# Building a kernel's rotation tables early, in bf16, and starting the first slab before the tables are complete

## The chip, the cores and the metric

The kernel runs on one core of one Trainium2 chip. The metric is the time of one execution on the device, in microseconds (us). The record marks each run as fast or slow; a run is slow when it is over 1.5% above the fastest of the same kernel.

The engines are called by the profile's short names: PE (TensorE, matrix multiplication), DVE (VectorE, elementwise work), ACT (ScalarE, activations), POOL (GpSimd) and SP (SyncE, used here for issuing DMA). The *span* is the time from the first to the last instruction of the profiled execution.

## The reference, cut to what matters

```python
def _A_ref(x, Lambda_re, Lambda_im, B_re, B_im, C_re, C_im, log_dt, Dskip):
    Lam = Lambda_re + 1j * Lambda_im
    dt = jnp.exp(log_dt)
    Lam_bar = jnp.exp(dt * Lam)                            # 512 complex factors
    B_bar = ((Lam_bar - 1.0) / Lam)[:, None] * (B_re + 1j * B_im)
    Bu = jnp.einsum("bld,pd->blp", x + 0j, B_bar)
    for t in range(L):                                     # L = 2048 steps
        h = Lam_bar[None, :] * h + Bu[:, t, :]
        ...
    return 2.0 * jnp.einsum("blp,dp->bld", hseq, Cmat).real + x * Dskip
def _B_ref(x, w_gate, w_up, w_down):                       # 512 -> 1376 -> 512
    return (_gelu(x @ w_gate) * (x @ w_up)) @ w_down

xn = _layernorm(x)                                         # x: 1 x 2048 x 512, bf16
return x + _A_ref(xn, ...) * _silu(_B_ref(xn, ...))
```

The complex recurrence is the sequential part. The kernel writes `Lam_bar` as a radius `rho` times a rotation. It rotates the inputs of each step backwards by the angle that has gathered, so that the scan itself is real with the factor `rho`, and rotates the results forwards again. For this it needs tables over the 512 positions of a slab: cosine and sine, and the same rotation multiplied by `2 (Lam_bar - 1) / Lam`, which is called `W`.

## The kernel before

The sequence is cut into four slabs of 512 positions. A prologue loads everything, computes the layernorm and builds the tables. Then, for each slab, eleven blocks of the feed-forward network (FFN) are interleaved with four scan groups, one for each 128 states. The cuts are marked with `# ...`.

```python
prolo_cm = tc.tile_pool(name="prolo", bufs=1)
prolo = prolo_cm.__enter__()                 # memory that is given back after the prologue
xT = prolo.tile([P, KT, S], BF16, name="xT")
# ... parameters, x (transposed while it is loaded) and the weights are fetched by DMA
for c in range(NSLAB):                       # layernorm statistics
    # ... mean_ps: matmuls of xT with ones
    x2 = prolo.tile([P, KT, TS], BF16, name="x2", tag="x2", bufs=2)
    nc.vector.tensor_tensor(out=x2[:], in0=xT[:, :, cols], in1=xT[:, :, cols], op=ALU.mult)
    # ... msq_ps: matmuls of x2 with ones; m2 = mean^2; var = msq - m2; mean_b; lnv; rstd_b
emit_xn(0)                                   # xnT = (xT - mean_b) * rstd_b, two DVE ops per 128x512
# ... dt_, th, a1, rho, c0, s0; then the 4-wide arithmetic that gives cr2, ci2
ang  = prolo.tile([P, NPT, TB], FP32, name="ang")        # TB = 64
ctab = prolo.tile([P, NPT, TS], FP32, name="ctab")
stab = prolo.tile([P, NPT, TS], FP32, name="stab")
# ... ctab, stab = sin/cos of ang for the first 64 columns, by ACT
while width < TS:                            # 64 -> 128 -> 256 -> 512 columns
    for pt in range(NPT):
        nc.vector.tensor_scalar(out=tmp_tab[:, 0:width], in0=stab[:, pt, 0:width], ...)
        nc.vector.scalar_tensor_tensor(out=ctab[:, pt, width : 2 * width], ...)
        nc.vector.tensor_scalar(out=tmp_tab[:, 0:width], in0=ctab[:, pt, 0:width], ...)
        nc.vector.scalar_tensor_tensor(out=stab[:, pt, width : 2 * width], ...)
    # ... the angle is doubled, width *= 2
nc.vector.tensor_copy(out=cos_b[:], in_=ctab[:])         # fp32 -> bf16, 128 x 2048
nc.vector.tensor_copy(out=sin_b[:], in_=stab[:])
for pt in range(NPT):                        # Wre_b and Wim_b, 512 columns each, from fp32
    # ... two tensor_scalar and two scalar_tensor_tensor
nc.vector.tensor_scalar(out=nWre_b[:], in0=Wre_b[:], scalar1=-1.0, ...)
nc.vector.tensor_scalar(out=nWim_b[:], in0=Wim_b[:], scalar1=-1.0, ...)
# ... diagI
for c in range(1, NSLAB):
    emit_xn(c)
prolo_cm.__exit__(None, None, None)          # the working pools below reuse prolo's memory
up  = ctx.enter_context(tc.tile_pool(name="up", bufs=4))
gel = ctx.enter_context(tc.tile_pool(name="gel", bufs=2))    # zb, sq, arg, sg, ub, zu
gp  = ctx.enter_context(tc.tile_pool(name="gp", bufs=2))     # fb, sf, g
# ... further working pools

def ffn_j(s, j, at):
    # ... g_ps: 4 matmuls
    nc.scalar.activation(out=zb[:fs], in_=g_ps[:fs, :], func=AF.Copy)
    nc.scalar.activation(out=sq[:fs], in_=g_ps[:fs, :], func=AF.Square, scale=math.sqrt(A_GELU))
    nc.vector.scalar_tensor_tensor(out=arg[:fs], in0=sq[:fs], scalar=1.0, in1=zb[:fs], ...)
    nc.scalar.activation(out=sg[:fs], in_=arg[:fs], func=AF.Sigmoid, scale=2.0 * C_GELU)
    # ... u_ps: 4 matmuls, ub = copy of it by ACT
    nc.vector.tensor_tensor(out=zu[:fs], in0=zb[:fs], in1=ub[:fs], op=ALU.mult)
    nc.vector.tensor_tensor(out=at[:fs, j, :], in0=sg[:fs], in1=zu[:fs], op=ALU.mult)

def down_m(s, m, at, gs, xs):
    # ... f_ps (2 buffers): 11 matmuls; xres is loaded
    nc.scalar.activation(out=fb[:], in_=f_ps[:, :], func=AF.Copy)
    nc.scalar.activation(out=sf[:], in_=f_ps[:, :], func=AF.Sigmoid)
    nc.vector.tensor_tensor(out=g[:], in0=fb[:], in1=sf[:], op=ALU.mult)
    gs.append(g)                             # y_epi reads g, after the y_ps matmuls

for s in range(NSLAB):
    for kind, idx in inter:                  # 3 FFN, scan, 3 FFN, scan, 3 FFN, scan, 2 FFN, scan
        if kind == "ssm":
            ssm_pt(s, idx, hst)              # p, wre, wim, fre, fim (scans), q, hst
        else:
            ffn_j(s, idx, at)
    # ... down_m and y_epi of the slab before
# ... down_m and y_epi of the last slab
```

## Time and profile before

| | kernel before |
|---|---|
| time, median of 5 runs | 286.31 us (285.25 to 286.47) |
| span of the profiled run | 283.0 us |
| DVE busy / idle in the span | 242.5 us / 40.5 us |
| first xnT written by DVE | 35.92 us |
| first FFN result zb on ACT | 72.64 us |
| last slab's scans done, g of the tail | 253.68 us |

The first view is the page's summary of the kernel before. Its first line gives busy microseconds, share of the span and instruction count for each engine. The rows of digits below it are the busy share in tenths, in 40 equal slices of 7.1 us.

```profile
PE 193.6 (68%) x880; PEld 85.4 (30%) x880; DVE 242.5 (86%) x610; ACT 145.7 (51%) x272; POOL 1.0 (0%) x8
...
PE   0058070000598898898898799789969988908993
...
DVE  0136499999699999999999999999999999999444
ACT  0218960000787585678576458757636697412420
```

DVE is full from the sixth slice to near the end, with a dip at 71 to 78 us (slice 11). It starts nearly empty, and PE and ACT stand still from about 42 to 73 us.

The second view, of the same kernel, is busy time by stage. The columns are the stretch in us, its length, then busy us and instruction count for PE, PEld, DVE, ACT and POOL, the granted PE clock, the DMA share and GB/s. The stages are: until the first xnT; the rest of the prologue; the body; the tail.

```profile
0.00:35.92 35.92, 9.98 (x32) 3.81 (x33) 11.37 (x36) 15.85 (x23) 0.98 (x8) 0.91 0.88 181
35.92:73.75 37.83, 5.35 (x16) 1.93 (x16) 36.78 (x123) 5.12 (x12) 0.00 (x0) 0.59 0.23 65
73.75:253.68 179.93, 155.47 (x716) 69.10 (x716) 177.29 (x423) 118.27 (x227) 0.00 (x0) 0.98 0.04 13
253.68:283.00 29.32, 22.78 (x116) 10.59 (x115) 17.09 (x30) 6.51 (x12) 0.00 (x0) 0.91 0.17 55
```

In the start DVE works for 11.4 of 35.9 us. In the second stage it is busy for 36.8 of 37.8 us, while PE and ACT do little. The body is DVE time, 177.3 of 179.9 us.

The third view is the timeline of DVE before, cut to the waits that matter: start, duration, engine and line, operation, result and sources, shapes, count, and in brackets the idle time just before it and what ended that.

```profile
18.90 2.36 DVE L125 TENSOR_TENSOR x<-xT 128x2048 bf16<-128x2048 bf16 x2 [10.20 <-DMA xT<-in_A_x_dram]
...
29.27 0.69 DVE L134 TENSOR_TENSOR var<-msq_ps,m 128x512 f32<-128x512 f32 x1 [2.88 <-ACT m L132]
...
35.92 0.76 DVE L150 TENSOR_TENSOR xnT<-xc,rstd_b 128x512 bf16<-128x512 bf16 x2 [3.76 <-ACT rstd_b L143]
...
71.66 0.74 DVE L290 SCALAR_TENSOR_TENSOR Wim_b<-stab,cr,wtmp 128x512 bf16<-128x512 f32 x1
...
73.75 0.69 DVE L410 SCALAR_TENSOR_TENSOR arg<-sq,zb 128x512 bf16<-128x512 bf16 x1 [0.63 <-ACT sq L408]
...
76.67 0.42 DVE L424 TENSOR_TENSOR at<-sg,zu 128x512 bf16<-128x512 bf16 x1 [1.89 <-ACT sg L414]
```

DVE stands idle for 10.2 us because x has not landed, while the table work that does not need x lies behind it in the program. At 71.66 us the last prologue operation runs that reads a tile of the prologue's pool; it ends at 72.40.

The fourth view is the first FFN activation on ACT, from the timeline of ACT before.

```profile
72.64 0.60 ACT L406 ACTIVATE zb<-g_ps 128x512 bf16<-128x512 f32 x1 [32.70 <-issue]
```

Its matmuls were done at about 41.7 us, yet zb came at 72.64, 0.24 us after the last read of the prologue's pool. The profile names no engine for the 32.7 us ("issue"). The reading is that the instruction waited for memory to come free; E2 below tests it.

### The profile page before, as it was taken

How to read it: one execution, taken by the hardware profiler on the slowest of the kernel's cores; microseconds unless marked ns; L12 is line 12 of the kernel's file. 1: busy time of each engine (PE TensorE's matmuls, PEld its weight loads, DVE VectorE, ACT ScalarE, POOL GpSimd, SP SyncE). 2: the span in 40 equal slices, each digit the busy share in tenths (PEclk: the TensorE clock that was granted, in tenths of full speed). 3: DMA queues.
4: the chain of work that ended last, by engine and by line, in shares of the span. 5: the costliest groups of instructions: out<-in, count | busy, mean ns of one | idle time of the engine just before them, and what ended most of it. 6: DMA issues, size and time to landing. Idle time of an engine off the chain costs nothing.

```text
span 283.0 us, 2919 instructions
## 1 busy us (share of the span) xinstructions
PE 193.6 (68%) x880; PEld 85.4 (30%) x880; DVE 242.5 (86%) x610; ACT 145.7 (51%) x272; POOL 1.0 (0%) x8
## 2 busy tenths in 40 slices
PE   0058070000598898898898799789969988908993
PEld 0013020000243343343353344334424433403441
DVE  0136499999699999999999999999999999999444
ACT  0218960000787585678576458757636697412420
POOL 1000000000000000000000000000000000000000
PEclk9999568555599999999999999999999999977999
DMA  7999448000000000000000040000004000001301
GB/s 81 283 234 208 95 108 257 0 0 0 0 5 0 0 0 0 2 0 1 0 2 1 0 127 22 2 0 0 0 2 140 9 0 0 3 0 37 111 21 57
DMA packets 26224, 12.81 MB, mean 45 GB/s; under 512 B 19712, under 2 KB 25184, under 8 KB 26208
## 3 DMA queue, kind: packets, MB, share of 16 engines
q1 hardware_dynamic: 21520, 10.17, 14.6%
q10 hardware_dynamic: 4688, 2.46, 3.9%
q8 instruction: 7, 0.11, 0.2%
q14 instruction: 9, 0.07, 0.1%
HBM read 6.33 MB, written 2.10 MB: 30 GB/s over the span
## 4 chain that ended last, share of the span: by engine, by line
DVE 53%; issue 16%; ACT 13%; PE 9%; DMA 6%; SPq 2%; ACTq 1%; DVEq 0%
DVE fre L360 7%; DVE fim L363 7%; DVE at L424 4%; DMA xT<-in_A_x_dram 4%; DVE arg L410 4%; PE y_ps L451 4%; DVE zu L423 4%; PE f_ps L435 4%; DVE p L344 2%; ACT zb L406 2%; ACT sg L414 2%; ACT ub L421 2%; DVE p L349 2%; DVE wre L345 2%; ACT sq L408 2%
## 5 line engine op out<-in xcount | busy, mean ns | idle before, releaser
L402 PE MATMUL g_ps<-xnT,wg 128*128 128x512 bf16 (+1 forms) x176 | 47.0, 389 | 49.7 <-ACT sq L408 39.3
L435 PE MATMUL f_ps<-wd,at 128*128 128x512 bf16 (+1 forms) x176 | 44.0, 385 | 13.0 <-ACT sf L441 11.7
L406 ACT ACTIVATE zb<-g_ps 128x512 bf16<-128x512 f32 (+1 forms) x44 | 26.7, 606 | 46.7 <-issue 32.7
L417 PE MATMUL u_ps<-xnT,wu 128*128 128x512 bf16 (+1 forms) x176 | 47.1, 390 | 4.2 <-ACT uim L339 3.7
L414 ACT ACTIVATE sg<-arg 128x512 bf16<-128x512 bf16 (+1 forms) x44 | 28.0, 636 | 28.6 <-DVE arg L410 28.4
L402 PEld LDWEIGHTS <-wg 128*128 128x128 bf16 (+1 forms) x176 | 17.7, 101 | 73.9 <-issue 57.1
L451 PE MATMUL y_ps<-C,hst 128*128 128x512 bf16 x128 | 31.7, 384 | 0.6 <-DVE hst L389 0.6
L410 DVE SCALAR_TENSOR_TENSOR arg<-sq,zb 128x512 bf16<-128x512 bf16 (+1 forms) x44 | 30.1, 684 | 0.8 <-ACT sq L408 0.6
L435 PEld LDWEIGHTS <-at 128*128 128x128 bf16 (+1 forms) x176 | 17.0, 98 | 34.0 <-DVE q L388 12.4
L421 ACT ACTIVATE ub<-u_ps 128x512 bf16<-128x512 f32 (+1 forms) x44 | 27.3, 620 | 0.0
L408 ACT ACTIVATE sq<-g_ps 128x512 bf16<-128x512 f32 (+1 forms) x44 | 26.8, 610 | 0.0
L417 PEld LDWEIGHTS <-wu 128*128 128x128 bf16 (+1 forms) x176 | 18.0, 102 | 26.7 <-issue 7.9
L439 ACT ACTIVATE fb<-f_ps 128x512 f32<-128x512 f32 x16 | 9.7, 604 | 23.1 <-DVE g L443 13.3
L424 DVE TENSOR_TENSOR at<-sg,zu 128x512 bf16<-128x512 bf16 (+1 forms) x44 | 18.6, 424 | 2.4 <-ACT sg L414 2.4
L423 DVE TENSOR_TENSOR zu<-zb,ub 128x512 bf16<-128x512 bf16 (+1 forms) x44 | 18.6, 422 | 0.0
L121 PE MATMUL mean_ps<-xT,onesK 128*128 128x512 bf16 x16 | 6.0, 499 | 17.0 <-DMA xT<-in_A_x_dram 17.0
L451 PEld LDWEIGHTS <-hst 128*128 128x128 bf16 x128 | 12.3, 99 | 14.9 <-issue 1.6
L326 PE MATMUL u_re_ps<-xnT,BreT 128*128 128x512 bf16 x64 | 16.5, 380 | 0.1
L332 PE MATMUL u_im_ps<-xnT,BimT 128*128 128x512 bf16 x64 | 16.4, 379 | 0.0
L363 DVE TENSOR_TENSOR_SCAN fim<-rho,init_im,wim 128x512 bf16<-128x512 f32 x12 | 15.4, 1282 | 0.0
L360 DVE TENSOR_TENSOR_SCAN fre<-rho,init_re,wre 128x512 bf16<-128x512 f32 x12 | 15.4, 1281 | 0.0
L463 DVE TENSOR_TENSOR yg<-y_ps,g 128x512 f32<-128x512 f32 x16 | 10.8, 688 | 5.3 <-PE y_ps L455 5.3
(111 smaller groups left out, 266.7 us busy)
## 6 DMA issues: line engine op xcount, KB each, us to landing
xres<-in_A_x_dram SPq DMA_DIRECT2D x16, 128.0 KB, 2.5
out_dram<-ot SPq DMA_DIRECT2D x16, 128.0 KB, 1.7
wu<-in_B_w_up_dram ACTq DMA_DIRECT2D x1, 1376.0 KB, 6.9
wg<-in_B_w_gate_dram SPq DMA_DIRECT2D x1, 1376.0 KB, 8.1
wd<-in_B_w_down_dram SPq DMA_DIRECT2D x1, 1280.0 KB, 7.0
wd<-in_B_w_down_dram SPq DMA_DIRECT2D x1, 96.0 KB, 6.7
BreT<-in_A_B_re_dram SPq DMA_TRANSPOSE x4, 6.2
BimT<-in_A_B_im_dram SPq DMA_TRANSPOSE x4, 2.7
```

The costliest lines, as they stand in the source:

```text
L360: nc.vector.tensor_tensor_scan(out=fre[:], data0=rho_b_ap, data1=wre[:], initial=ire, op0=ALU.mult, op1=ALU.add)
L363: nc.vector.tensor_tensor_scan(out=fim[:], data0=rho_b_ap, data1=wim[:], initial=iim, op0=ALU.mult, op1=ALU.add)
L402: nc.tensor.matmul(g_ps[:fs, :], lhsT=wg[:, kt, fsl], rhs=xnT[:, kt, cols], start=(kt == 0), stop=(kt == KT - 1))
L406: nc.scalar.activation(out=zb[:fs], in_=g_ps[:fs, :], func=AF.Copy)
L408: nc.scalar.activation(out=sq[:fs], in_=g_ps[:fs, :], func=AF.Square, scale=math.sqrt(A_GELU))
L410: nc.vector.scalar_tensor_tensor(out=arg[:fs], in0=sq[:fs], scalar=1.0, in1=zb[:fs], op0=ALU.add, op1=ALU.mult)
L414: nc.scalar.activation(out=sg[:fs], in_=arg[:fs], func=AF.Sigmoid, scale=2.0 * C_GELU)
L417: nc.tensor.matmul(u_ps[:fs, :], lhsT=wu[:, kt, fsl], rhs=xnT[:, kt, cols], start=(kt == 0), stop=(kt == KT - 1))
L421: nc.scalar.activation(out=ub[:fs], in_=u_ps[:fs, :], func=AF.Copy)
L423: nc.vector.tensor_tensor(out=zu[:fs], in0=zb[:fs], in1=ub[:fs], op=ALU.mult)
L435: nc.tensor.matmul(f_ps[:, :], lhsT=at[:fs, k, m0 : m0 + P], rhs=wd[:fs, k, :], start=(k == 0), stop=(k == NFT - 1))
L451: nc.tensor.matmul(y_ps[:, :], lhsT=hst[:, j, m0 : m0 + P], rhs=C2[:, j, :], start=(j == 0), stop=False)
```

## The change

The intent is to use the time in which DVE waits for x, and not to let the first slab wait for the tables. The change has five parts.

1. The parameters come first and the table work is written ahead of the statistics. Fences (`issue_after`) keep the scheduler to this order on ACT and DVE.
2. The tables are bf16 from the start. `cos`, `sin`, `-Wre` and `-Wim` are all doubled from 64 to 512 columns, instead of building `W` at 512 columns from fp32 `cos` and `sin`, casting, and negating. `Wre` itself is no longer needed: `q1` gets the other sign, and an addition becomes a subtraction.
3. The table tiles no longer lie in the prologue's pool, so they don't hold its memory.
4. The remaining doublings are written after slab 0's eleven FFN blocks, and slab 0's four scan groups follow.
5. The activations are grouped by function (Exp, Sin, Ln, Exp), which cuts ACT's table loads from 8 to 5.

```diff
+        nc.sync.dma_start(out=pb[:, 2 * NPT : 3 * NPT], in_=A_log_dt.rearrange(...))
         nc.sync.dma_start(out=pb[:, NPT : 2 * NPT], in_=A_Lambda_im.rearrange(...))
         ...
+    def emit_tables_early():
+        # dt_, th, a1, rho, c0, s0, then m2cr, m2ci (= -2 times what cr2, ci2 held), ang: as before, but in consts
+        nc.scalar.activation(out=cos_b[:, :, 0:TB], in_=ang[:], func=AF.Sin, bias=halfpi[:], scale=1.0)
+        nc.scalar.activation(out=sin_b[:, :, 0:TB], in_=ang[:], func=AF.Sin)
+        # nWre_b, nWim_b at 64 columns: 16 small operations
+        tmpA = consts.tile([P, TS // 2], BF16, name="tmpA")
+        tmpB = consts.tile([P, TS // 2], BF16, name="tmpB")
+        pairs = [(cos_b, sin_b, tmpA), (nWre_b, nWim_b, tmpB)]
+        def double_to(limit):
+            ...                      # the loop of before, for both pairs, in bf16
+        double_to(2 * TB)
+        last_dve = nc.cur_bb.bb.instructions[-1]
+        return double_to, last_act, last_dve
+    double_to, last_act, last_dve = emit_tables_early()
+    def emit_tables_late():
+        double_to(TS)
+        ...                          # diagI
     for c in range(NSLAB):
         ...
-        nc.vector.tensor_tensor(out=x2[:], in0=xT[:, :, cols], in1=xT[:, :, cols], op=ALU.mult)
+        with tc.issue_after(last_dve):
+            nc.vector.tensor_tensor(out=x2[:], in0=xT[:, :, cols], in1=xT[:, :, cols], op=ALU.mult)
         ...                          # Ln, Exp and Copy regrouped with issue_after
     emit_xn(0)
-    ...                              # the old table code in prolo, cast, W builds, negations, diagI
     for c in range(1, NSLAB):
         emit_xn(c)
     prolo_cm.__exit__(None, None, None)
     ...
-        nc.vector.tensor_tensor(out=q1[:], in0=Wre_b[:, pt, :], in1=fre[:], op=ALU.mult)
+        nc.vector.tensor_tensor(out=q1[:], in0=nWre_b[:, pt, :], in1=fre[:], op=ALU.mult)
         nc.vector.tensor_tensor(out=q2[:], in0=nWim_b[:, pt, :], in1=fim[:], op=ALU.mult)
-        nc.vector.tensor_tensor(out=hst[:, pt, :], in0=q1[:], in1=q2[:], op=ALU.add)
+        nc.vector.tensor_tensor(out=hst[:, pt, :], in0=q2[:], in1=q1[:], op=ALU.subtract)
     ...
+        if s == 0:
+            for j in range(NFT):
+                ffn_j(0, j, at)
+            emit_tables_late()
+            for pt in range(NPT):
+                ssm_pt(0, pt, hst)
+        else:
             for kind, idx in inter:
                 ...
```

## The prediction

> **What bounds it now.** The stretch table (busy time by window) shows VectorE busy for 10.0, 9.7 and 9.9 us of the three 10 us windows from 40 to 70, 19.85 of 20 from 80 to 100, and 50.00 of 50 in each window from 100 to 250. So: a start (first xnT write at 35.9 us), a VectorE-bound body to 253.8, a TensorE tail of 29 us. From 35.9 to 73.75 the body is prologue. The wait view has one 32.7 us wait of ScalarE before the first zb, labelled "issue", and one 32 us wait of TensorE for sq. I read it as the prologue pool's memory: the working tiles reuse it, so the first zb must wait until the last prologue tile (tables, xT) has been read.
>
> **What changes, on VectorE.**
> Start-to-start costs read from the timeline: 512-wide bf16 tensor_tensor 0.335 us, scalar_tensor_tensor 0.20/0.26/0.39/0.66 at 64/128/256/512, fp32 tensor_scalar 0.16/0.19/0.26/0.40.
> - The 37.8 us from 35.9 to 73.75 holds 30 layernorm operations (10.1 us, kept) and 27.7 us of table work, small operations and a 0.6 us wait.
> - After: the tables at 64 and 128 columns are made while VectorE waited for x and statistics. What must be done late is 19 of 32 operations at 128 columns (3.9 us), 32 at 256 (8.8) and small ones (1.3): 14 us. This uses about 0.17 us for a 256-wide bf16 tensor_scalar, an estimate from the Trainium skill, "VectorE: DVE Perf Modes", side-by-side table (four elements per cycle; the trace's 2048-wide bf16 negation, 0.69 us, agrees).
> - The late tables no longer sit in the prologue pool, so its memory comes free at the last xnT, about 46 us, and slab 0's FFN (11 x 1.28 = 14.1 us of VectorE) runs among the table work.
>
> **The start.** ScalarE's table loads fall from 8 to 5 at 1.28 us each (Trainium skill, "ScalarE: Activation LUTs", what a load costs: 1283 ns; trace agrees). But early tables occupy VectorE until about 23.4 us, so the squares of x start there, not at 18.9. I expect this to cancel: first rstd near 35.5, first xnT after the statistics near 36 (35.9 before).
>
> **Sum.** 36.2 + 10.1 (layernorm) + 14.0 (tables) + 14.1 (FFN 0) + 1.5 bubbles (cold TensorE clock, sigmoid load) = 75.9 us, when slab 0's scans begin. Before, the body after 73.75 lasted 180.0 us, with 2.5 of start bubbles and 14.1 of slab 0's FFN: 163.4 remain, so the body ends at 239.3; plus the unchanged 29.2 tail gives a span of 268.5, some 14.5 us less. Nearly all is on the critical path: VectorE is saturated. Predicted time 271.8 us, range 267 to 276.5. Chances: faster by over 2% 0.95, within 2% 0.04, slower 0.01.
>
> **What would show it.** First zb near 46 us instead of 72.6; the 32 us waits gone; TensorE busy from 46 on; VectorE busy total lower by 8 to 14 us; first xnT near 36; VectorE saturated from about 36 to 239; tail 29 us.
>
> **What would make it wrong.** (a) Early tables delay the statistics more than the saved table loads help: first xnT at 38 to 40 costs that much one for one. (b) Slab 0's FFN alone, with two buffers and in-order table work between arg, zu and at, or a cold TensorE, leaves VectorE idle for more than 1.5 us. (c) The four scan groups in a row starve on f_ps or on ure/uim. (d) bf16 tensor_scalar with a per-partition scalar runs slower than assumed (up to 2 us). (e) The tail grows through a lower clock.

## The result, and the profile after

| | before | after |
|---|---|---|
| time, median (range, runs) | 286.29 us (285.25 to 287.17, 16) | 267.51 us (266.08 to 268.59, 9) |
| span of the profiled run | 283.0 us | 265.5 us |
| DVE busy / idle in the span | 242.5 / 40.5 us | 242.4 / 23.1 us |
| first xnT / first zb | 35.92 / 72.64 us | 33.64 / 43.95 us |
| g of the tail, and from there to the end | 253.68 / 29.3 us | 234.78 / 30.7 us |

The ratio of the times is 0.9351, with a 95% interval from 0.9331 to 0.9370. A ratio in this document is the record's ratio of one kernel's fast runs to those of the kernel before in the same rounds. It differs from the ratio of the medians quoted by up to 0.0007.

The summary of the page after, with the same rows as before:

```profile
PE 198.1 (75%) x880; PEld 86.8 (33%) x880; DVE 242.4 (91%) x654; ACT 142.1 (53%) x269; POOL 1.0 (0%) x8
...
PE   0037372999988658996987998797799789239992
...
DVE  0699999999999999999999999999999999997254
ACT  0605823999474406577474748666458758130410
```

Read the two DVE entries side by side. The busy time is the same to 0.1 us, 242.5 against 242.4; the row of digits is full from the third slice (6.6 us each) instead of the sixth. So the 17.5 us of span are idle time of DVE that is gone (40.5 - 23.1 = 17.4), not work that is gone.

Busy time by stage after. The stages are: until the first xnT; the layernorm; late tables with slab 0's FFN; the body from the first scan operation of slab 0; the tail.

```profile
0.00:33.64 33.64, 8.84 (x32) 3.48 (x33) 24.01 (x112) 14.34 (x26) 0.98 (x8) 1.00 0.85 187
33.64:43.70 10.06, 5.27 (x16) 1.96 (x16) 10.06 (x31) 1.52 (x3) 0.00 (x0) 0.83 0.56 135
43.70:71.75 28.05, 26.04 (x111) 11.30 (x111) 28.05 (x95) 25.41 (x49) 0.00 (x0) 0.94 0.15 49
71.75:234.78 163.03, 133.77 (x607) 59.03 (x606) 163.03 (x394) 94.27 (x180) 0.00 (x0) 0.96 0.05 14
234.78:265.50 30.72, 24.18 (x116) 11.08 (x115) 17.26 (x30) 6.51 (x12) 0.00 (x0) 0.88 0.17 52
```

The start is 2.3 us shorter and holds 24.0 us of DVE work instead of 11.4: the 12.6 us more, nearly all table work, were fitted in where DVE had waited. The idle time of DVE in the start falls from 24.55 to 9.63 us, so 14.9 of the 17.4 us are here: 12.6 filled with work and 2.3 from the shorter start. From 33.64 to 234.78 DVE has no idle time at all. Until the end of the tables, without the 14.1 us of slab 0's FFN, DVE does 24.01 + 10.06 + 28.05 - 14.1 = 48.0 us of work after, and 11.37 + 36.78 = 48.2 us before.

The timeline of DVE after, at the places shown of before:

```profile
21.59 1.23 DVE L274 TENSOR_TENSOR x<-xT 128x2048 bf16<-128x2048 bf16 x1
...
25.23 0.70 DVE L284 TENSOR_TENSOR var<-msq_ps,m 128x512 f32<-128x512 f32 x1
...
33.64 0.76 DVE L302 TENSOR_TENSOR xnT<-xc,rstd_b 128x512 bf16<-128x512 bf16 x2 [1.01 <-ACT rstd_b L292]
...
43.03 0.76 DVE L302 TENSOR_TENSOR xnT<-xc,rstd_b 128x512 bf16<-128x512 bf16 x2
...
45.07 0.69 DVE L409 SCALAR_TENSOR_TENSOR arg<-sq,zb 128x512 bf16<-128x512 bf16 x1
...
47.99 0.42 DVE L423 TENSOR_TENSOR at<-sg,zu 128x512 bf16<-128x512 bf16 x1
```

The waits of 10.20, 2.88, 0.63 and 1.89 us are gone, and that for rstd fell from 3.76 to 1.01. The pool's last reader is now the last xnT, which ends at 43.79, and the timeline of ACT shows the first zb 0.16 us after it:

```profile
43.95 0.60 ACT L405 ACTIVATE zb<-g_ps 128x512 bf16<-128x512 f32 x1 [8.79 <-issue]
```

Why is the busy time the same, although the large fp32 operations are gone? The groups of DVE instructions by line answer it. The columns are line, operation, names, shapes, count, busy us, mean ns and idle time before. These are three of the table groups before:

```profile
L232 DVE SCALAR_TENSOR_TENSOR ctab<-ctab,cw,tmp_tab 128x64 f32<-128x64 f32 (+2 forms) x12 | 4.6, 380 | 0.1
L225 DVE TENSOR_SCALAR tmp_tab<-stab,sw 128x64 f32<-128x64 f32 (+2 forms) x12 | 3.7, 306 | 0.1
...
L283 DVE SCALAR_TENSOR_TENSOR Wre_b<-ctab,cr,wtmp 128x512 bf16<-128x512 f32 x4 | 3.0, 748 | 0.0
```

And these are two of the groups after, the same step of a doubling:

```profile
L223 DVE SCALAR_TENSOR_TENSOR cos_b<-cos_b,cw,tmpA 128x64 bf16<-128x64 bf16 (+2 forms) x12 | 4.5, 374 | 0.0
...
L219 DVE TENSOR_SCALAR tmpA<-sin_b,sw 128x64 bf16<-128x64 bf16 (+2 forms) x12 | 3.1, 261 | 0.0
```

In bf16 the scalar_tensor_tensor of a doubling costs what it cost in fp32 (374 against 380 ns on average); only the tensor_scalar got cheaper (261 against 306). But twice as many tables are doubled, 96 operations instead of 48. The sum of the table groups' durations was 16.6 (doublings) + 9.8 (W) + 2.4 (casts) + 1.4 (negations) = 30.2 us before, and is 30.4 (doublings) + 4.2 (W at 64 columns) = 34.6 us after. Neighbouring instructions overlap in these sums, by about 0.09 us whatever their width: at 64 columns a tensor_scalar lasts 0.24 us and the next one starts after 0.15, at 512 columns a build of `W` lasts 0.75 and the next starts after 0.67. There are 112 table operations after and 68 before, so overlap takes back about 4 us of the 4.4 us that the sums differ by (44 x 0.09, an estimate), and DVE's time comes out nearly even.

Finally the gap of PE at the head of the tail, in the timeline of PE before:

```profile
255.53 1.87 PE L435 MATMUL f_ps<-wd,at 128*128 128x512 bf16 x4 [7.89 <-ACT sf L441]
257.29 2.39 PE L451 MATMUL y_ps<-C,hst 128*128 128x512 bf16 x8
```

and in the timeline of PE after:

```profile
236.62 1.86 PE L434 MATMUL f_ps<-wd,at 128*128 128x512 bf16 x4 [8.97 <-ACT sf L440]
238.38 3.57 PE L450 MATMUL y_ps<-C,hst 128*128 128x512 bf16 x8
```

After a longer gap the same eight matmuls take 3.57 instead of 2.39 us. From 5 to 10 us after the tail's g the granted clock is 0.75 after and 1.00 before. The tail's 116 matmuls keep PE busy for 24.18 instead of 22.78 us, which is the tail's extra 1.4 us.

### The profile page after: what moved, and what is told of

Read it like the earlier page. It is cut to its first block, busy times and chain, and to the rows that moved or that the text cites. A ratio compares the mean times of both kernels' runs of the same rounds, so it can differ in the third digit from the quotient of the medians.

```text
span 265.5 us, 2957 instructions
## 1 busy us (share of the span) xinstructions
PE 198.1 (75%) x880; PEld 86.8 (33%) x880; DVE 242.4 (91%) x654; ACT 142.1 (53%) x269; POOL 1.0 (0%) x8
## 4 chain that ended last, share of the span: by engine, by line
DVE 73%; PE 9%; ACT 8%; issue 4%; ACTq 3%; DMA 1%; DVEq 0%
DVE fim L362 7%; DVE fre L359 7%; DVE arg L409 6%; DVE at L423 5%; DVE zu L422 5%; PE y_ps L450 5%; PE f_ps L434 4%; ACTq L82 3%; DVE p L343 2%; DVE xnT L302 2%; DVE p L349 2%; DVE p L348 2%; DVE wre L344 2%; DVE q L386 2%; DVE g L442 2%
## 5 line engine op out<-in xcount | busy, mean ns | idle before, releaser
L401 PE MATMUL g_ps<-xnT,wg 128*128 128x512 bf16 (+1 forms) x176 | 48.6, 397 | 20.0 <-ACT sq L407 13.2
L434 PE MATMUL f_ps<-wd,at 128*128 128x512 bf16 (+1 forms) x176 | 45.4, 387 | 18.8 <-ACT sf L440 12.2
L450 PE MATMUL y_ps<-C,hst 128*128 128x512 bf16 x128 | 34.8, 414 | 0.9 <-DVE hst L388 0.9
L407 ACT ACTIVATE sq<-g_ps 128x512 bf16<-128x512 f32 (+1 forms) x44 | 26.7, 607 | 0.0
L438 ACT ACTIVATE fb<-f_ps 128x512 f32<-128x512 f32 x16 | 9.6, 598 | 27.1 <-DVE g L442 14.1
L269 PE MATMUL mean_ps<-xT,onesK 128*128 128x512 bf16 x16 | 5.1, 472 | 19.0 <-DMA xT<-in_A_x_dram 17.8
L450 PEld LDWEIGHTS <-hst 128*128 128x128 bf16 x128 | 13.0, 105 | 16.5 <-issue 4.0
L337 ACT ACTIVATE ure<-u_re_ps 128x512 bf16<-128x512 f32 x16 | 9.7, 604 | 15.1 <-PE u_re_ps L325 7.9
L462 DVE TENSOR_TENSOR yg<-y_ps,g 128x512 f32<-128x512 f32 x16 | 10.7, 687 | 7.0 <-PE y_ps L454 7.0
```

What stands on the lines that cost most here:

```text
L401: nc.tensor.matmul(g_ps[:fs, :], lhsT=wg[:, kt, fsl], rhs=xnT[:, kt, cols], start=(kt == 0), stop=(kt == KT - 1))
L434: nc.tensor.matmul(f_ps[:, :], lhsT=at[:fs, k, m0 : m0 + P], rhs=wd[:fs, k, :], start=(k == 0), stop=(k == NFT - 1))
L450: nc.tensor.matmul(y_ps[:, :], lhsT=hst[:, j, m0 : m0 + P], rhs=C2[:, j, :], start=(j == 0), stop=False)
```

## The experiments

Two theories fit the profile after, and the prediction had made a third:

- IDLE: DVE paces the kernel, and the gain is the idle time at its start that is now filled with table work.
- OVERLAP: the gain is that ACT and PE start slab 0 about 28 us earlier, because the pool's memory comes free at 43.8 instead of 72.4 us.
- LESS WORK: the gain is that the new tables cost DVE fewer microseconds. The prediction's expected fall of DVE's busy total says this, though its sum does not rest on it.

All eight kernels gave correct results. Each was timed in three rounds (four runs each, with the profiled one) beside the kernel before, which had medians of 285.71 us (E1 to E4) and 286.41 us (E4b to E7).

### E1: the early tables without the early start of slab 0

In the changed kernel the late doublings are written before the prologue's pool is closed, two of their tiles are put back into that pool, and slab 0 gets the mixed order of the other slabs.

```diff
-        tmpA = consts.tile([P, TS // 2], BF16, name="tmpA")
-        tmpB = consts.tile([P, TS // 2], BF16, name="tmpB")
+        tmpA = prolo.tile([P, TS // 2], BF16, name="tmpA")
+        tmpB = prolo.tile([P, TS // 2], BF16, name="tmpB")
     ...
+    emit_tables_late()
     prolo_cm.__exit__(None, None, None)
     ...
-        if s == 0: ... else: ...
+        for kind, idx in inter: ...      # slab 0 like the others
```

> The changed kernel with all of its table work before the prologue pool closes (the two doubling temporaries lie in that pool, the late tables are emitted before it is released, slab 0 uses the old mixed order), so ScalarE and TensorE wait for the tables again, as they did in the kernel before; VectorE's work is the same. Theory IDLE (VectorE paces the body; what the change won is VectorE idle time in the start, filled with table work): only the start-up bubbles of about 3 us come back, 269.5 to 272 us, ratio to before about 0.945, VectorE busy 242. Theory OVERLAP (what the change won is that ScalarE and TensorE start slab 0 some 28 us earlier): most of the 18.8 us is lost, 280 us or more.

Measured: 272.35 us (271.52 to 273.46), ratio 0.9539 (0.9496 to 0.9581), span 269.9 us. The start is the same as in the changed kernel (squares at 21.57, first xnT at 33.61). The timelines of ACT and DVE of this kernel show that the wait for the pool is back, and so are the bubbles (short waits of DVE) at the start of slab 0, while PE runs at 0.50 of its clock (57.5 to 62.5 us) and ACT loads the sigmoid's table (59.92 us):

```profile
57.84 0.60 ACT L406 ACTIVATE zb<-g_ps 128x512 bf16<-128x512 f32 x1 [22.70 <-issue]
```

```profile
58.95 0.69 DVE L410 SCALAR_TENSOR_TENSOR arg<-sq,zb 128x512 bf16<-128x512 bf16 x1 [0.86 <-ACT sq L408]
...
61.87 0.43 DVE L424 TENSOR_TENSOR at<-sg,zu 128x512 bf16<-128x512 bf16 x1 [1.89 <-ACT sg L414]
```

What follows: 13.1 of the 17.5 us of span come without any early start of slab 0. ACT waits 22.7 us for the pool, and the span is only 4.4 us longer than that of the changed kernel, 3.5 of them such bubbles on DVE (some smaller ones beside the two shown). The time is 0.35 us over the upper end of what IDLE expected and 7.6 us under what OVERLAP expected.

### E2: the early start of slab 0 without the early tables

In the kernel before, all tiles of the table work are moved out of the prologue's pool; nothing else is changed.

```diff
-    ctab = prolo.tile([P, NPT, TS], FP32, name="ctab")
-    stab = prolo.tile([P, NPT, TS], FP32, name="stab")
+    ctab = consts.tile([P, NPT, TS], FP32, name="ctab")
+    stab = consts.tile([P, NPT, TS], FP32, name="stab")
     # ... likewise iota_i, iota_f, ang, thT, cw, sw, tmp_tab, sq_tmp, wtmp
```

> The kernel before with every table tile moved out of the prologue pool, nothing else: the first zb no longer waits for the tables, only for the last read of xT. VectorE's work and its start are unchanged. IDLE: only the 3 us of start-up bubbles in VectorE's stream go, 282.5 to 285 us. OVERLAP: most of the gain appears here, 275 us or less.

Measured: 280.21 us (279.65 to 280.59), ratio 0.9802 (0.9774 to 0.9830), span 278.8 us. The first zb is at 53.47 us, 0.16 us after the pool's last reader (an xnT that ends at 53.31), in the timeline of ACT:

```profile
53.47 0.60 ACT L406 ACTIVATE zb<-g_ps 128x512 bf16<-128x512 f32 x1 [13.70 <-issue]
```

The stretch from 54 to 80 us in the table of busy time by stage, first for the kernel before and then for this one (DVE is the third of the busy columns):

```profile
54.00:80.00 26.00, 6.23 (x20) 2.35 (x20) 22.50 (x47) 7.33 (x14) 0.00 (x0) 0.55 0.00 0
```

```profile
54.00:80.00 26.00, 16.88 (x55) 6.48 (x57) 25.86 (x56) 12.37 (x23) 0.00 (x0) 0.69 0.00 1
```

What follows: PE does 10.7 us more in this stretch and ACT 5.0 us more, and the span gains 4.2 us, of which 3.4 are the idle time of DVE that goes away in this very stretch. Both theories missed the time: IDLE expected 282.5 us or more, so it is off by over 2 us, OVERLAP by over 5. The early start is worth about 2% (1.7 to 2.3% by the interval).

E1 and E2 are the two halves of the change, and their ratios multiply to 0.9539 x 0.9802 = 0.935, which is the ratio of the whole change, 0.9351. In spans, 13.1 + 4.2 = 17.3 of 17.5 us. E1's half still holds several parts together: the early tables, their bf16 arithmetic and the grouped activations.

### E3: the new tables, but little of them early

In the changed kernel, `W` at 64 columns and the first doubling are moved to the late part; the squares of x no longer wait for them.

```diff
+        last_dve = nc.cur_bb.bb.instructions[-1]     # now right after thT
-        double_to(2 * TB)
-        last_dve = nc.cur_bb.bb.instructions[-1]
     def emit_tables_late():
+        build_w()                                    # nWre_b, nWim_b at 64 columns
         double_to(TS)
```

> The changed kernel with the W tables at 64 columns and the doublings to 128 taken out of the start and made late; the grouped Exp, Sin, Ln, Exp order of ScalarE stays. About 8.5 us of VectorE work (14.2 to 21.5 and a little more) leave the time in which it would wait for x. IDLE: squares of x start near 18 instead of 21.6, first xnT 2.5 to 3.5 us earlier (near 30.5), body 8 us longer: 271 to 274 us. Theory LESS WORK (as the prediction had it: fewer VectorE microseconds in the tables is the gain, their place is not): within 1 us of the changed kernel or faster, 264 to 268.5 us.

Measured: 273.22 us (272.38 to 273.97), ratio 0.9558 (0.9523 to 0.9593), span 270.5 us. DVE is busy for 241.6 us, 0.8 less than in the changed kernel, and the kernel is still 5.0 us of span longer. The squares of x and the first xnT come earlier (18.41 and 31.16 us), and the wait for x is back in the timeline of DVE:

```profile
18.41 2.36 DVE L276 TENSOR_TENSOR x<-xT 128x2048 bf16<-128x2048 bf16 x2 [7.60 <-DMA xT<-in_A_x_dram]
```

What follows: the same arithmetic in the same precision loses 5 us when it isn't in the window where DVE waits for x. LESS WORK expected at most 268.5 us and falls; IDLE expected 271 to 274 and holds. But E3 also keeps 12.5 of the 17.5 us of span, and not all of that is the pool of E2. Its squares start only 0.5 us before those of the kernel before (18.41 and 18.90 us), yet its first xnT comes 4.8 us earlier (31.16 and 35.92 us). Between the two, ACT loads tables twice in E3, and five times at 1.28 us in the kernel before. So writing the parameters' activations first and grouping them (parts 1 and 5) is a likely source of some 4 us, and would also explain why the early tables did not delay the first xnT. No run tests it alone.

### E4 and E4b: the old arithmetic in the new places

E4 takes the changed kernel and puts the old fp32 arithmetic into it. `ctab` and `stab` are doubled to 256 columns early; the last doubling, the casts, the four `W` builds and the two negations come late, and all their tiles lie outside the prologue's pool.

```diff
-        pairs = [(cos_b, sin_b, tmpA), (nWre_b, nWim_b, tmpB)]
+        pairs = [(ctab, stab, tmpA)]                 # fp32
-        double_to(2 * TB)
+        double_to(4 * TB)
     def emit_tables_late():
         double_to(TS)
+        build_w()                                    # casts, W at 512 columns, negations
```

> The changed kernel's placement with the old table algorithm: fp32 cosine and sine doubled to 256 columns early, the last doubling, two casts, four W builds and two negations late. VectorE's table work in the two traces has about the same sum. IDLE: VectorE busy 242 to 245 us, 266 to 270 us. LESS WORK: the fp32 tables cost 10 us or more, 277 us or more, with VectorE busy 10 us higher than in the changed kernel.

Measured: 275.74 us (275.51 to 276.04), ratio 0.9648 (0.9622 to 0.9673), span 273.4 us: between the two expectations. The experiment was spoiled. The scheduler put the first subtraction of the layernorm ahead of early doublings, and DVE stood idle for 6.7 us until its mean was there:

```profile
21.55 0.43 DVE L310 TENSOR_TENSOR xc<-xT,mean_b 128x512 bf16<-128x512 bf16 x1 [6.69 <-ACT mean_b L304]
```

E4b repairs this with one more fence.

```diff
-            nc.vector.tensor_tensor(out=xc[:], in0=xT[:, kt, cols], in1=mean_b[:, c, :], op=ALU.subtract)
+            with tc.issue_after(last_dve):
+                nc.vector.tensor_tensor(out=xc[:], in0=xT[:, kt, cols], in1=mean_b[:, c, :], op=ALU.subtract)
```

> The run with the old fp32 table algorithm in the new placement, with the mean subtractions held behind the early doublings, so that VectorE no longer sits idle for 6.7 us in the start. IDLE: VectorE busy again 242 to 243.5, span shorter by 5 to 6.7 us than without the fence, so 269 to 271 us. LESS WORK: the earlier 275.7 was the price of the fp32 tables, so 274.5 us or more.

Measured: 272.37 us (271.68 to 273.78), ratio 0.9517 (0.9475 to 0.9558), span 270.6 us: again between the two, 1.4 us above what IDLE expected and 2.1 below what LESS WORK expected. DVE is busy for 243.0 us, only 0.6 more than with the new arithmetic. The other 4.5 of the 5.1 us of span are idle time, and the largest new piece of it is in the start, in the timeline of DVE:

```profile
19.40 1.23 DVE L283 TENSOR_TENSOR x<-xT 128x2048 bf16<-128x2048 bf16 x1 [0.36 <-DMA xT<-in_A_x_dram]
...
25.28 0.69 DVE L293 TENSOR_TENSOR var<-msq_ps,m 128x512 f32<-128x512 f32 x1 [3.06 <-PE msq_ps L286]
```

What follows: the old arithmetic itself is hardly dearer for DVE. The 3.06 us are not a lack of early table work either: right after the wait, at 25.89 us, DVE goes on with doublings at 128 columns whose inputs had been ready before it. They stand behind `var` in DVE's order, as the scheduler left it. So E4b, too, carries a wait that is not the arithmetic's. The old arithmetic does leave its casts and `W` builds for late, since they need the finished tables, while the new one can start on `W` at 64 columns before x is there; what that is worth by itself these runs do not show.

### E5: four buffers for the tail

The tail grew by 1.4 us, and PE was idle for 9.0 us just before it. Does this gap set the tail's length? The chain, as read from the timelines: the third f_ps waits for sf, which frees an f_ps buffer; the next fb and sf on ACT wait for a `g` on DVE, since `gp` has two buffers; and that `g` comes late in DVE's order, after the last scan. E5 gives `gp` four buffers.

```diff
-    gp = ctx.enter_context(tc.tile_pool(name="gp", bufs=2))
+    gp = ctx.enter_context(tc.tile_pool(name="gp", bufs=4))
```

> The changed kernel with four buffers instead of two for fb, sf and g. In the trace of the changed kernel TensorE is idle from 227.6 to 236.6 us, because f_ps waits for sf, sf for fb's buffer and fb for g, which VectorE reaches only after its last scan. If that is the tail's length, TensorE does some 25 down-projection products in that gap and the tail after VectorE's last g of slab 2 falls from 30.7 to 23 to 25 us: 259.5 to 262.5 us. If the tail is set by TensorE's own work and clock after the last scan, no change within 1 us, 266.5 to 268.5.

Measured: 262.54 us (261.13 to 264.01), ratio 0.9170 (0.9128 to 0.9211). The profiled run was the slowest of the four and has a span of 262.2 us. Its start is the same code as in the changed kernel, but eight mean matmuls on PE took 3.57 instead of 1.89 us there, and its first xnT came at 34.91 instead of 33.64 us. So between single profiles, differences of about 1 us in the start mean little. The timeline of PE of this kernel:

```profile
225.46 3.40 PE L434 MATMUL f_ps<-wd,at 128*128 128x512 bf16 x15
230.16 1.25 PE L434 MATMUL f_ps<-wd,at 128*128 128x512 bf16 x5 [1.29 <-DVE at L423]
...
237.91 3.15 PE L434 MATMUL f_ps<-wd,at 128*128 128x512 bf16 x7 [5.20 <-ACT sf L440]
```

What follows: 22 matmuls of the tail, counting two at 232.10, move into the gap. From g at 236.01 to the end it is 26.2 us instead of 30.7. That is less gain than the 23 to 25 us expected, as a gap of 5.2 us before the second pair of f_ps remains; the time is at the upper end of the 259.5 to 262.5 us expected. The two buffers were a limit, but not the only one in this chain: the fb before that gap still waits for a `g` on DVE.

### E6: all transposed loads of x on the SP queue

In the changed kernel ACT issues two of the four transposing loads of x and the load of `wu`, which keeps it from its first table load until 8.31 us.

```diff
-        eng = nc.sync if kt % 2 == 0 else nc.scalar
+        eng = nc.sync
     ...
-    nc.scalar.dma_start(out=wu[:], in_=B_w_up.rearrange("(k p) f -> p k f", p=P))
+    nc.sync.dma_start(out=wu[:], in_=B_w_up.rearrange("(k p) f -> p k f", p=P))
```

> The changed kernel with all four transposes of x and the load of w_up issued from the SyncE queue, so that ScalarE's first table load (at 8.3 us in the changed kernel, behind its DMA issues) can run at once. Theory: the start is a chain from the parameters through ScalarE to the early tables, so the first rho moves from 10.1 to about 5.5 us and the squares of x from 21.6 to 18 to 19: 264 to 266 us. Rival: x itself (17.8 us) or its slower issue from one queue sets the start: no gain or a loss, 267 to 270 us.

Measured: 266.06 us (265.38 to 266.58), ratio 0.9291 (0.9265 to 0.9316), against 0.9351 for the changed kernel. The timeline of ACT of this kernel:

```profile
0.73 1.28 ACT L131 ACT_TABLE_LOAD   x1 [0.73 <-PEq L522]
3.67 0.20 ACT L131 ACTIVATE dt__138<-log_dt 128x4 f32<-128x4 f32 x1 [1.66 <-DVE log_dt L103]
7.60 0.21 ACT L136 ACTIVATE rho<-a 128x4 f32<-128x4 f32 x1 [3.72 <-DVE a L135]
```

What follows: the table load does come at 0.73 us, as expected, but then rho waits for the next parameters to land. The squares of x start at 21.43 us, where 18 to 19 had been expected. The first xnT is at 34.19 us; the changed kernel's start gave 33.64 and, in E5's profile, 34.91, so one profile cannot show a gain here. The small gain of about 0.6% does not come in the way that was expected, and its cause stays open.

### E7: E5 and E6 together

```diff
-        eng = nc.sync if kt % 2 == 0 else nc.scalar
+        eng = nc.sync
-    nc.scalar.dma_start(out=wu[:], ...)
+    nc.sync.dma_start(out=wu[:], ...)
-    gp = ctx.enter_context(tc.tile_pool(name="gp", bufs=2))
+    gp = ctx.enter_context(tc.tile_pool(name="gp", bufs=4))
```

> The two edits together (four buffers, all loads on SyncE). One is in the start, the other in the tail, so if both gain, the gains should add within 1 us: 256 to 260 us. If either does nothing alone, it should do nothing here.

Measured: 261.59 us (261.45 to 261.71), ratio 0.9136 (0.9118 to 0.9154), span 259.9 us. It has the lowest median of all the kernels, 2.3% under the changed one by the two ratios (0.9136 / 0.9351 = 0.977).

What follows: the 256 to 260 us expected were missed by 1.6 us, as E5 had gained less than hoped. If the gains of E5 and E6 added up, the ratio would be 0.9170 x 0.9291 / 0.9351 = 0.9111; measured is 0.9136, which is 0.7 us longer, so they add within the 1 us expected. But the intervals of E7 and E5 overlap, so these runs do not show clearly that E6's edit still helps beside E5's.

### All spans as DVE busy and DVE idle

| kernel | span | DVE busy | DVE idle |
|---|---|---|---|
| before | 283.0 | 242.5 | 40.5 |
| E2, early start alone | 278.8 | 241.6 | 37.2 |
| E4, old arithmetic, without the fence | 273.4 | 242.6 | 30.8 |
| E3, little of the tables early | 270.5 | 241.6 | 28.9 |
| E4b, old arithmetic, with the fence | 270.6 | 243.0 | 27.6 |
| E1, early tables alone | 269.9 | 243.2 | 26.7 |
| after | 265.5 | 242.4 | 23.1 |
| E6 | 264.8 | 242.2 | 22.6 |
| E5 | 262.2 | 242.6 | 19.6 |
| E7 | 259.9 | 242.3 | 17.6 |

All values are in us and come from the profiled runs; idle is the span less the busy time. Over ten kernels the busy time moves by 1.6 us and the span by 23.1 us. What separates these kernels is how long DVE waits.

## Why the prediction was right or wrong, point by point

The predicted time was 271.8 us in a range of 267 to 276.5; measured were 267.51 us. It was in the range, 0.5 us above its lower end, and the direction and its chance were right. There is some luck in this: without the 1.5 us by which the tail grew against the forecast, the time would have been about 266.0 us, under the range.

- **What bounds the kernel.** Right. The body is DVE time, and the wait of zb is the prologue's pool. In four kernels with different last readers of that pool, zb came 0.16 to 0.24 us after the last read (72.40 and 72.64; 43.79 and 43.95; 57.68 and 57.84 in E1; 53.31 and 53.47 in E2).
- **Layernorm, late tables and FFN of slab 0.** Right. Predicted were 10.1 us, then 14.0 + 14.1 us; measured were 10.06 and 28.05 us. The first zb came at 43.95 us, where about 46 had been expected. For the 256-wide bf16 tensor_scalar the prediction took 0.17 us, an estimate from the Trainium skill, "VectorE: DVE Perf Modes" (side-by-side table, four elements per cycle). The trace shows a duration of 0.29 us and 0.195 us from start to start, so a little more; with 16 such operations that is within 0.5 us.
- **The step that failed: "VectorE busy total lower by 8 to 14 us".** It is 242.5 before and 242.4 us after. The prediction had counted correctly that only 14 of 27.7 us of table work stay on DVE's path after the layernorm, and it said itself that the early tables are made while DVE waits. The 8 to 14 us fit the difference, 13.7 us, taken for work that disappears. The runs show that it was moved: DVE does 12.6 us more before the first xnT, in time that it had spent waiting for x and the statistics. The sum in the prediction did not use this total, so the mechanism behind the time was right and this sign of it was wrong. E3 shows the cost of the mistake: whoever believes in less work would expect E3 at 268.5 us or less, and it took 273.22.
- **The start.** Mis-sized. The sum took 36.2 us for the first xnT; measured were 33.64 us, so 2.6 us are from here. Of these, 1.8 us come from the squares of x, which start at 21.59 instead of 23.4 us. Three of the 32 doublings at 64 columns run only after the first squares (at 22.72, 24.05 and 24.54 us), which is about 0.55 us. The costs from start to start, 0.15 us (tensor_scalar) and 0.195 us (scalar_tensor_tensor) at 64 columns, are close to the 0.16 and 0.20 that the prediction had read. How it came to 23.4 us stays open. The other 0.8 us lie between the squares and the first xnT, and are less than the 1.3 us by which E5's profile of the same code differs. "I expect this to cancel" was too cautious by these amounts. ACT's table loads did fall from 8 to 5, at 1.28 us each.
- **Bubbles at the start of slab 0.** Predicted 1.5 us, measured none: the late table operations fill them. E1, where they are not there to do so, has 3.5 us.
- **The body.** Predicted 163.4 us, measured 163.0 us.
- **The tail.** Predicted 29.2 us, "unchanged"; measured 30.7. PE was idle for 8.97 instead of 7.89 us before it, and then ran at the lower clock for longer: at a granted clock of 0.50 and about 0.43 us per 512-wide matmul for some 5.7 us, against some 2.8 us before (estimates from the granted clock in windows of 0.5 us). This agrees with the two states of the Trainium skill, "TensorE: Matmul & The Clock Gate", Part 1 (half rate after idling, full rate after a window of activity of about 3.4 us, at a moment that varies), though neither 2.8 nor 5.7 us is that window. Why the cold stretch was the longer one in just this profile is not settled; reason (e) of what could make the prediction wrong did come true, for 1.5 us.
- **From span to time.** The prediction added 3.3 us, the difference between the median time and the span of the profiled run. But the profiled run of the kernel before was its fastest one, and its median less this span overstates the offset; after the change the same difference is 2.0 us (267.51 less 265.5). This is 1.3 us.

The terms add up to the miss of 4.3 us: 2.6 (start) + 1.5 (bubbles) + 0.4 (body) - 1.5 (tail) + 1.3 (offset) = 4.3.

What stays open is the share of the grouped activations, what the new arithmetic is worth beside its place, the cause of E6's small gain, and why E2 gained 0.9 us of DVE busy time beyond the bubbles.

## What to carry to other kernels

When one engine paces the kernel, read its idle time at the start as a place to put work in, and split work that is independent of the late input so that as much as possible of it can run there; write the account as busy and idle of that engine, because "less work" and "moved work" can forecast the same time and give different advice for the next step, as E3 showed. A pool that is closed after a prologue is a barrier for whatever reuses its memory: look for a long wait with no engine named, ending just after the pool's last read. Here that barrier alone was worth 2%, as the pacing engine was busy behind it, and four buffers in `gp` instead of two took off another 2% at the end. Before you credit one part of such a change, look for what else changed with it: here the grouped activations were never tested alone.

## What the Trainium skill lacked or had wrong

- "ScalarE: Activation LUTs", what a table load costs: it gives about 1283 ns for the load plus about 1380 ns of drain. The 1.28 us agree. The drain isn't seen in the traces here: after the change a zb ends at 46.02 us, the load runs from 46.03 to 47.31, and the sigmoid starts at 47.33.
- The same page, section on table sets: it says that ln followed by exp takes one load, as one set has both. In these kernels the Ln of the variance and the Exp of rstd each got a load of their own, at 22.61 and 31.68 us after the change, with only Square and Copy between them. Why the common set was not taken is not shown.
- "VectorE: DVE Perf Modes", table of tiers: it has no row for scalar_tensor_tensor, which carries most of the table work and the GELU here. In bf16 it took 684 ns at 512 columns, 486 at 256, 350 at 128 and 286 at 64; in fp32 at 256 columns it took 482, so bf16 gained it nothing.
- The same page, side-by-side table: an estimate from it for a 256-wide bf16 tensor_scalar at four elements per cycle, (64 + 8 + 150) / 0.96, is 231 ns; the duration was 284 to 289 ns. From start to start, which is what a row of them costs, it was 0.195 us for these, and 0.15 us at 64 columns, where the duration was 0.24 us.
